# Two-layer decode attention and gated feed-forward on one core: products that nobody reads between the last values and behind them, a scaling in four pieces, row means summed beside a transpose, and 2 KB more of values kept per partition

## The chip, the cores and the metric

One NeuronCore of a Trainium2 chip runs the whole program in one launch. The metric is the device time of that launch in microseconds (us), the median of several executions. TensorE (PE in the profile) multiplies, VectorE (DVE) does elementwise work and 32x32 block transposes, ScalarE (ACT) the exponential, GpSimd (POOL) a power, and SyncE (SP) issues nearly all DMA loads.

## The reference

Two layers of the same two blocks share one set of weights and one key and value cache. There are 2 batch rows of one token, 32 query heads on 8 key/value heads of width 128, and 32768 cached positions.

```python
D, Hq, Hkv, Sk, Dh, F = 512, 32, 8, 32768, 128, 1792
def _A_ref(x, k_cache, v_cache, wq, wo):
    q = (x @ wq).reshape(B, 1, Hq, Dh).transpose(0, 2, 1, 3)
    scores = einsum("bhqd,bhkd->bhqk", q, repeat(k_cache)) * (Dh ** -0.5)
    o = einsum("bhqk,bhkd->bhqd", softmax(scores), repeat(v_cache))
    return o.transpose(0, 2, 1, 3).reshape(B, 1, Hq * Dh) @ wo
def _B_ref(x, W_gate, W_up, W_down):
    gate, up = x @ W_gate, x @ W_up
    return (gate * (gate > 0) * up) @ W_down
for layer in range(2):
    x = x + _A_ref(_layernorm(x), k_cache, v_cache, wq, wo)
    x = x + _B_ref(_layernorm(x), W_gate, W_up, W_down)
```

All arrays are f32. Keys and values are 268 MB each and are read in both layers, so that 1.1 GB pass through the DMA queues.

## The kernel before

A "head" of the kernel is one pair of key/value head and batch row: NG = 16 of them. Layer 0 goes through them upward, layer 1 downward, so that the last head of layer 0 is the first of layer 1. For each head `keys` takes 8 pages of 128x4096 keys through `k_tile` into scores, `soft_max` and `soft_tail` make weights of them, and `values` takes 8 pages of values through `v_tile` into the PSUM tile `acc`. A page of values is 8 products of 512 columns. They are written to four strips of 32 partitions of `acc` (`32 * c`), four products at a time, one for each strip. Each f32 product stands twice in a trace, since TensorE runs it in two passes.

Behind the last value of a head `evacuate` (L316) scales `acc` by one over the sum; `head_out` (L327) turns it by four small products into the tile `po` and copies it to `oT`; `project` (L338) multiplies by `wo` into `op`. Behind the last head of a layer the chain goes on: `add` (L175) forms the residual and its row sums, `centred` (L144) subtracts the mean, transposes and squares, `factor` (L156) makes the inverse deviation, and `feed_forward` (L354) multiplies by the gate and up weights (`wgu`, eight loads of 896 KB in layer 0), then by `wd`. Layer 1 begins with `queries` (L182) and eight loads of `wq`.

All loads go into one area `arena` of 220 units of 1 KB per partition (128 KB over the 128 partitions). `take` (L62) gives a load the free units that were set free first, at multiples of 8 units for the sizes here; `done` marks units as free in program order, and the load that gets them waits on the chip for the instruction that read them last. SP issues in program order, so a load that waits holds up all loads behind it.

At the end of layer 0 the area is nearly full: the 8 key pages of the last head (128 units) and of its values the pages 4 to 6 and the last quarter of page 3 (52 units) stay for layer 1, which does not load them again. `KEPT_PART, KEPT_FROM = 3, 6` says that page 3 is loaded as blocks 0 to 5 and blocks 6 and 7, and that the second part stays. Page 7 comes in four quarters. 40 units are left for all loads up to the first keys of layer 1. By `take`'s rule these make four slots of 8 units that rotate: the first four `wgu` loads get one each, and each later `wgu`, `wd` and `wq` load waits for the products on the load four places ahead of it. The first slots are those of page 3's first part (first `wgu` load), of the third and fourth quarter of page 7 (second), of the weights `pT` and of page 7's second quarter (third), and of `wo` (fourth).

Of the kernel before, what the change touches and what calls it, by code (L numbers as in the profile page):

```python
# [8 lines left out]
F32 = mybir.dt.float32  # L9
AF = mybir.ActivationFunctionType  # L10
ALU = mybir.AluOpType
AX = mybir.AxisListType
# [23 lines left out]


KEPT_PAGES = (4, 5, 6)
KEPT_PART, KEPT_FROM = 3, 6
DOWN = (4, 4, 2, 2, 1, 1)  # L40


SIDE_HEAD, SIDE_PAGE, SIDE_AT, SIDE = 12, 5, 4, 3
SIDE_ROWS, SIDE_CHUNKS = 20, 5

C_SAME, C_MEAN, C_SELH, C_PAIR, C_COL, C_SELQ, C_SIDE, C_END = 0, 128, 256, 272, 304, 306, 338, 339


@with_exitstack
def attention_reglu_decode(ctx: ExitStack, tc: tile.TileContext, x, k, v, side, wq, wo, wgu, wd, consts, out):  # L50
# [23 lines left out]
    def load(src, top=False):  # L74
        t = take(src.shape[-1], top, False)
        nc.sync.dma_start(t[0], src)
        return t

    def done(loaded):
        clock[0] += 1  # L80
        for u in loaded[1]:
            freed[u] = clock[0]
# [27 lines left out]
    selh = cst[:, C_SELH : C_SELH + 16]  # L110
    pair = cst[:, C_PAIR : C_PAIR + 32]
    selq = cst[:, C_SELQ : C_SELQ + 32]
    mean_rows = cst[:, C_MEAN : C_MEAN + P]
    side_rows = cst[:, C_SIDE : C_SIDE + 1]
    col = cst[:, C_COL : C_COL + NB]

# [13 lines left out]
    def small(name):  # L130
        return ps.tile([P, D], F32, tag="small", bufs=2, name=name)
# [1 line left out]
    ring = sb.tile([P, 32], F32, name="stat")  # L133
    turn = [0]

    def one(n=1):
        at = turn[0]
        turn[0] = (at + 2) % 32
        return ring[:, at : at + n]

    def centred(total, name):  # L144
        mp = small(f"mean{name}")
        nc.tensor.matmul(mp[:, 0:1], mean_rows, total, start=True, stop=True)  # L146
        work, xT = take(2 * P), take(P)
        xc, sq = work[0][:, :P], work[0][:, P:]
        nc.vector.tensor_scalar(xc, xq, mp[:, 0:1], None, ALU.subtract)
        nc.vector.transpose(xT[0], xc)  # L150
        ss = one()
        nc.vector.scalar_tensor_tensor(sq, xc, 1.0, xc, ALU.mult, ALU.mult, accum_out=ss)
        done(work)
        return xT, xT[0].rearrange("p (a b) -> p a b", b=32), ss

    def factor(ss, name, by_row):  # L156
        vp = small(f"var{name}")
        n = 1 if by_row else NB
        ve, rs = one(NB), one(NB)
        if by_row:  # L160
            nc.tensor.matmul(vp[:, :n], mean_rows, ss, start=True, stop=True)
        else:
            sc = one(NB)
            nc.vector.tensor_scalar_mul(sc, col, ss[:, 0:1])
            nc.tensor.matmul(vp[:, :n], mean_cols.to_broadcast([P, P]), sc, start=True, stop=True)
        nc.vector.tensor_scalar_add(ve[:, :n], vp[:, :n], EPS)
        nc.gpsimd.tensor_tensor(rs[:, :n], ve[:, :n], mhalf[:, :n], ALU.pow)
        return rs

# [4 lines left out]

    def add(tot):  # L175
        total = one()
        nc.vector.scalar_tensor_tensor(xq, tot[:, :P], 1.0, xq, ALU.mult, ALU.add, accum_out=total)
        return total


# [1 line left out]
    def queries(L, total, first, between):  # L182
        xt, xT, ss = centred(total, f"a{L}")
        qp = ps.tile([P, 2, D], F32, tag="sc", bufs=2, name=f"qp{L}")
        rq = one(NB)
        front = first // (NG // 2)
        order = [B * KT + kt for B in (front, 1 - front) for kt in range(KT)]
        parts = blocks(wq, 4 * D, order, 1 if L else 2 * KT)
        for B in (front, 1 - front):
            for kt in range(KT):  # L190
                t = next(parts)
                for c in range(4):
                    nc.tensor.matmul(qp[32 * c : 32 * c + 32, B, :], xT[:, kt, :], t[0][:, c * D : (c + 1) * D],  # L193
                                     start=kt == 0, stop=kt == KT - 1)
                done(t)
                if B != front and kt:
                    next(between, None)
                if B == front and kt == 0:
                    nc.vector.tensor_scalar_mul(rq, factor(ss, f"a{L}", False), DH ** -0.5)
            q = take(D)  # L200
            qs = q[0].rearrange("p (a b) -> p a b", b=32)
            nc.vector.transpose(q[0], qp[:, B, :])
            for b in range(NB):
                nc.vector.tensor_scalar_mul(qT[:, 16 * B : 16 * B + 16, b], qs[:, :, b], rq[:, b : b + 1])
            done(q)
            if B == front:
                place_queries(0, first)
        done(xt)
# [21 lines left out]

    def soft_max(L, n):
        m1 = one()
        nc.vector.tensor_reduce(m1, sc_of[n], AX.XY, ALU.max)  # L233
        mp = small(f"mp{L}_{n}")
        mt = take(32)
        nc.vector.tensor_scalar_mul(mt[0], pair, m1[:, 0:1])  # L236
        nc.tensor.matmul(mp[:, :32], same, mt[0], start=True, stop=True)  # L237
        done(mt)
        nm = one()
        nc.vector.tensor_reduce(nm, mp[:, :32], AX.X, ALU.max, negate=True)  # L240
        p = take(2 * D)
        rs = one()
        nc.scalar.activation(p[0], sc_of[n].rearrange("p a b -> p (a b)"), AF.Exp, bias=nm[:, 0:1], scale=1.0, accum_out=rs)  # L243
        red_of[n] = (p, rs)

    def soft_tail(L, n, aside=False):
        p, rs = red_of.pop(n)
        pT = take(2 * D)
        for B in range(2):
            nc.vector.transpose(pT[0][:, B * D : (B + 1) * D], p[0][:, B * D : (B + 1) * D])  # L250
        if aside:
            side_of[n] = side_keys(p[0])
        done(p)
        sm = small(f"sm{L}_{n}")
        nc.tensor.matmul(sm[:, 0:1], same, rs, start=True, stop=True)  # L255
        linv = one()
        nc.vector.reciprocal(linv, sm[:, 0:1])  # L257
        pT_of[n], linv_of[n] = pT, linv


# [39 lines left out]
    def v_tile(n, j, vt, first, last, blocks):  # L300
        pT = pT_of[n][0].rearrange("p (b m r) -> p b m r", m=16, r=32)
        parts = 4 // len(blocks) if len(blocks) < 4 else 1
        for at, ch in enumerate(blocks):
            J, B, m = j // 4, j // 2 % 2, j % 2 * 8 + ch
            for e in range(parts):
# [5 lines left out]
                    start=first and ch < 4, stop=last and blocks[-1] == 7 and at >= len(blocks) - 4,  # L311
                )

    acs_of = {}

    def evacuate(L, n, split):  # L316
        done(pT_of.pop(n))
        acs_of[n] = take(D)
        acs = acs_of[n][0]
        linv = linv_of.pop(n)  # L320
        if split:
            nc.vector.tensor_scalar_mul(acs[:, : D // 2], acc[:, : D // 2], linv[:, 0:1])  # L322
            nc.scalar.activation(acs[:, D // 2 :], acc[:, D // 2 :], AF.Copy, scale=linv[:, 0:1])
        else:
            nc.vector.tensor_scalar_mul(acs, acc, linv[:, 0:1])  # L325

    def head_out(L, n):  # L327
        acs = acs_of.pop(n)
        po = small(f"po{L}_{n}")
        for t in range(4):  # L330
            nc.tensor.matmul(po[:, :REP], acs[0][:, t * P : (t + 1) * P], selh[:, 4 * t : 4 * t + 4],  # L331
                             start=t == 0, stop=t == 3)
        done(acs)
        nc.vector.tensor_copy(oT[:, :, n % NB], po[:, :REP])  # L334

# [62 lines left out]
        return add(tot)  # L398

    total = one()  # L400
    nc.vector.tensor_reduce(total, xq, AX.X, ALU.add)
    kept_k, kept_v = [], []
    for L in range(NLAYER):
        last = L == NLAYER - 1
# [29 lines left out]
        def values(i, soft):  # L434
# [18 lines left out]
            for at, (j, lo, hi, t) in enumerate(pieces):  # L453
                if i == SIDE_HEAD and j == HALF:
                    aside = take(2 * SIDE_CHUNKS * D, False, False)
                    sides = load_side(L, aside)
                next(sides, None)
                next(sides, None)
                if i == SIDE_HEAD and j == NT - 1:
                    v_side(n, aside[0])  # L460
                    done(aside)
                t = t or next(whole, None) or load(v[n, j // HALF, :, j % HALF * PAGE + lo * D : j % HALF * PAGE + hi * D])
                v_tile(n, j, t[0], at == 0, j == NT - 1, range(lo, hi))
                if not last and i == NG - 1 and (j in KEPT_PAGES or j == KEPT_PART and lo):
                    kept_v.append((j, lo, hi, t))
                else:
                    done(t)
                if soft is not None and at == 0:
                    soft_max(L, soft)
            evacuate(L, n, i == NG - 1)  # L470

        first_keys = keys(0)
# [8 lines left out]
        values(NG - 1, None)  # L481
        head_out(L, seq[NG - 1])
        project(load(wo[seq[NG - 1] // NB]), NG)
        total = feed_forward(L, add(op))
    nc.sync.dma_start(out, xq)

# [58 lines left out]
```

## Time and profile before

| | us |
|---|---|
| median of 3 runs | 2578.14 (2577.77 to 2578.51) |
| the profiled execution | 2580.14 |
| its span, first to last instruction | 2578.3 |

The profiled execution stands 2.00 us above the median of the timed runs and 1.84 us above its own span. In the profile, PE is the matmul part of TensorE and PEld its weight loads; SPq is SyncE's issue of DMAs; PEclk is the share of the full 2.4 GHz that TensorE was granted, 1.00 or 0.50 at an instant and a mean over a stretch.

### The profile page before, as it was taken

Reading aid. Unit: us, or ns where it says so; the run is one execution under the profiler, and the core shown is the slowest. Engines: PE = TensorE matmul, PEld = TensorE weight load, DVE = VectorE, ACT = ScalarE, POOL = GpSimd, SP = SyncE. Lnnn points to the kernel's source line nnn. Section 1 sums busy time; section 2 is a strip of 40 time slices with the busy share of each in tenths; the row PEclk is TensorE's granted clock in tenths of the full one; section 3 lists DMA queues with packets and bytes.
Section 4 is the critical chain, followed back from the end, with each engine's and each line's share of the span. In section 5 each row is a group of like instructions: output and inputs, shape, how many; then the busy total and the mean of one; then the engine's idle time right before and its main releaser. Section 6 shows DMA issues by size and latency. Waiting matters only on the chain.

```text
span 2578.3 us, 19563 instructions
## 1 busy us (share of the span) xinstructions
PE 1306.9 (51%) x9264; PEld 337.3 (13%) x9264; DVE 147.5 (6%) x351; ACT 42.1 (2%) x69; POOL 3.4 (0%) x13
## 2 busy tenths in 40 slices
PE   2444454455445544645575554445445544554456
PEld 0111111111111111111121111111111111111111
DVE  0000000000000000000010000000000000000000
ACT  0000000000000000000000000000000000000000
POOL 0000000000000000000000000000000000000000
PEclk9777777777776777777878777767777777777778
DMA  9999999999999999999999999999999999999999
GB/s 426 427 435 435 431 432 435 431 436 431 429 439 430 431 437 429 421 436 421 424 403 434 435 434 433 434 429 435 434 428 436 434 425 440 434 431 422 436 422 391
DMA packets 31919, 1107.34 MB, mean 429 GB/s; under 512 B 3600, under 2 KB 3984, under 8 KB 7440
## 3 DMA queue, kind: packets, MB, share of 16 engines
q1 hardware_dynamic: 31552, 1105.87, 99.7%
q8 instruction: 72, 1.18, 0.2%
q10 hardware_dynamic: 288, 0.24, 0.0%
q14 instruction: 7, 0.06, 0.0%
HBM read 1106.03 MB, written 0.07 MB: 429 GB/s over the span
## 4 chain that ended last, share of the span: by engine, by line
DMA 69%; PE 22%; another core or an unknown queue 9%; issue 0%; DVE 0%; SPq 0%; ACTq 0%; DVEq 0%
DMA arena<-k 54%; PE sc L223 15%; DMA arena<-v 11%; PE acc L307 4%; DMA cst<-consts 2%; DMA arena<-wd 1%; DMA arena<-wq 1%; PE po L331 1%; PE qp L193 1%; PE op L344 0%; DMA arena<-wgu 0%; PE mp L237 0%; PE gu L362 0%; PE sm L255 0%
## 5 line engine op out<-in xcount | busy, mean ns | idle before, releaser
L223 PE MATMUL sc<-arena,qz 128*32 128x512 f32 x4096 | 592.5, 731 | 597.8 <-DMA arena<-k 597.8
L307 PE MATMUL acc<-arena 128*16 128x512 f32 (+1 forms) x4136 | 584.6, 717 | 591.8 <-DMA arena<-v 591.8
L223 PEld LDWEIGHTS sc<-arena,qz 128*32 128x32 f32 x4096 | 144.5, 131 | 1000.5 <-issue 690.5
L307 PEld LDWEIGHTS acc<-arena 128*16 128x16 f32 x4136 | 118.3, 108 | 1007.9 <-issue 506.2
L233 DVE TENSOR_REDUCE stat<-sc 128x1 f32<-128x1024 f32 x32 | 39.2, 1225 | 646.0 <-PE sc L223 646.0
L243 ACT ACTIVATE arena<-sc,stat 128x1024 f32<-128x1024 f32 x32 | 35.7, 1115 | 2372.5 <-DVE stat L240 2319.6
L325 DVE TENSOR_SCALAR arena<-acc,stat 128x512 f32<-128x512 f32 x30 | 22.5, 751 | 719.9 <-PE acc L307 719.9
L250 DVE STREAM_TRANSPOSE arena<-arena 128x512 f32<-128x512 f32 x64 | 41.5, 687 | 2.5 <-ACT arena L243 2.5
L331 PE MATMUL po<-cst,arena 128*128 128x4 f32 x256 | 34.7, 258 | 2.4 <-DVE arena L322 1.2
L331 PEld LDWEIGHTS po<-cst,arena 128*128 128x128 f32 x256 | 31.9, 195 | 27.1 <-issue 23.5
L257 DVE RECIPROCAL stat<-sm 128x1 f32<-128x1 f32 x32 | 5.3, 166 | 436.2 <-PE sm L255 436.2
L240 DVE TENSOR_REDUCE stat<-mp 128x1 f32<-128x32 f32 x32 | 6.1, 192 | 360.6 <-PE mp L237 360.6
L362 PE MATMUL gu<-arena 128*32 128x448 f32 x128 | 20.5, 751 | 12.2 <-DMA arena<-wgu 11.4
L193 PE MATMUL qp<-arena 128*32 128x512 f32 x128 | 22.1, 801 | 5.9 <-DMA arena<-wq 3.5
L146 PE MATMUL meana<-stat,cst 128*128 128x1 f32 x4 | 0.9, 304 | 43.4 <-DMA cst<-consts 43.0
L237 PEld LDWEIGHTS mp<-arena,cst 128*128 128x128 f32 x64 | 13.3, 260 | 52.5 <-issue 45.8
L237 PE MATMUL mp<-arena,cst 128*128 128x32 f32 x64 | 17.3, 358 | 3.3 <-DVE arena L236 3.3
L344 PE MATMUL op<-arena,oT 128*2 128x512 f32 x112 | 14.6, 592 | 3.6 <-DVE oT L334 3.6
L255 PEld LDWEIGHTS sm<-stat,cst 128*128 128x128 f32 x64 | 9.5, 188 | 28.8 <-issue 28.8
L255 PE MATMUL sm<-stat,cst 128*128 128x1 f32 x64 | 12.2, 260 | 0.0
L334 DVE COPY oT<-po 128x4 f32<-128x4 f32 x32 | 5.2, 161 | 78.0 <-PE po L331 78.0
L384 PE MATMUL dn<-arena 128*32 128x512 f32 x32 | 6.4, 894 | 4.3 <-DVE arena L373 3.2
(62 smaller groups left out, 85.7 us busy)
## 6 DMA issues: line engine op xcount, KB each, us to landing
arena<-v SPq DMA_DIRECT2D x31, 2048.0 KB
arena<-wo SPq DMA_DIRECT2D x16, 1024.0 KB
arena<-k SPq DMA_DIRECT2D x8, 2048.0 KB
arena<-wq SPq DMA_DIRECT2D x8, 1024.0 KB
arena<-wgu SPq DMA_DIRECT2D x8, 896.0 KB
arena<-wgu SPq DMA_DIRECT2D x4, 1792.0 KB
arena<-v SPq DMA_DIRECT2D x9, 512.0 KB
arena<-wd SPq DMA_DIRECT2D x4, 1024.0 KB
```

Source lines behind the costliest of these rows:

```text
L193: nc.tensor.matmul(qp[32 * c : 32 * c + 32, B, :], xT[:, kt, :], t[0][:, c * D : (c + 1) * D], start=kt == 0, stop=kt == KT - 1)
L223: nc.tensor.matmul(sc_of[n][32 * c : 32 * c + 32, B, :], qz[:, i % 2, 28 - 4 * j : 60 - 4 * j], kt[:, ch * D : (ch + 1) * D], start=j == 0 ...
L233: nc.vector.tensor_reduce(m1, sc_of[n], AX.XY, ALU.max)
L237: nc.tensor.matmul(mp[:, :32], same, mt[0], start=True, stop=True)
L243: nc.scalar.activation(p[0], sc_of[n].rearrange("p a b -> p (a b)"), AF.Exp, bias=nm[:, 0:1], scale=1.0, accum_out=rs)
L250: nc.vector.transpose(pT[0][:, B * D : (B + 1) * D], p[0][:, B * D : (B + 1) * D])
L255: nc.tensor.matmul(sm[:, 0:1], same, rs, start=True, stop=True)
L307: nc.tensor.matmul(acc[32 * c : 32 * c + 16, e * w : (e + 1) * w], pT[:, B, m, 16 * J : 16 * J + 16], vt[:, at * D + e * w : at * D + (e + ...
L325: nc.vector.tensor_scalar_mul(acs, acc, linv[:, 0:1])
L331: nc.tensor.matmul(po[:, :REP], acs[0][:, t * P : (t + 1) * P], selh[:, 4 * t : 4 * t + 4], start=t == 0, stop=t == 3)
L344: nc.tensor.matmul(op[32 * u : 32 * u + NB, :], oT[:, u, :], w, start=i == 3, stop=i == NG - 1)
L362: nc.tensor.matmul(gu[32 * j : 32 * j + 32, s, :FS], xT[:, kt, :], t[0][:, j * FS : (j + 1) * FS], start=kt == 0, stop=kt == KT - 1)
```

## The change

Six edits stand in it. `KEPT_FROM` goes from 6 to 5: page 3 is split after block 4, its second part (6 units instead of 4) is kept, and layer 1 loads 2 units less. `keep_busy(n, w)` is new: it issues n products of `same[:, :32]` with w columns of the first kept key page into a PSUM tile `hot` that nothing reads, always on partitions 0 to 31. It works only in layer 0, from page 4 of the last head's values on: four products of 512 columns behind each of the pages 4, 5 and 6, two of 256 behind each of the first three quarters of page 7, and one or two of 256 at four places from the last quarter on up to `centred`, which ends it. `evacuate` scales the last head's values in four pieces of 128 columns on DVE instead of two halves on DVE and ACT. `centred` and `factor` sum by column: the mean comes as a 128x2 product while DVE transposes x, and subtraction and squares work on 128x8 elements. The constants lose the 128 columns of `mean_rows`. The temporaries of `one` are all two columns wide.

```diff
-KEPT_PART, KEPT_FROM = 3, 6
+KEPT_PART, KEPT_FROM = 3, 5
...
     def centred(total, name):
         mp = small(f"mean{name}")
-        nc.tensor.matmul(mp[:, 0:1], mean_rows, total, start=True, stop=True)
-        work, xT = take(2 * P), take(P)
-        xc, sq = work[0][:, :P], work[0][:, P:]
-        nc.vector.tensor_scalar(xc, xq, mp[:, 0:1], None, ALU.subtract)
-        nc.vector.transpose(xT[0], xc)
-        ss = one()
-        nc.vector.scalar_tensor_tensor(sq, xc, 1.0, xc, ALU.mult, ALU.mult, accum_out=ss)
-        done(work)
-        return xT, xT[0].rearrange("p (a b) -> p a b", b=32), ss
+        tm, xT, sq, ss = one(), take(P), take(KT * NB), one()
+        xv = xT[0].rearrange("p (a b) -> p a b", b=32)
+        nc.vector.tensor_scalar_mul(tm, col, total[:, 0:1])
+        nc.tensor.matmul(mp[:, :NB], mean_cols.to_broadcast([P, P]), tm, start=True, stop=True)
+        keep_busy(1)
+        hot.clear()
+        nc.vector.transpose(xT[0], xq)
+        mean = bass.AP(mp.tensor, mp.offset, [mp.ap[0], [0, KT], [1, NB]])
+        nc.vector.tensor_tensor(xv[:, :, :NB], xv[:, :, :NB], mean, ALU.subtract)
+        nc.vector.tensor_tensor(sq[0].rearrange("p (a b) -> p a b", b=NB), xv[:, :, :NB], xv[:, :, :NB], ALU.mult)
+        nc.vector.tensor_reduce(ss, sq[0].rearrange("p (a b) -> p b a", b=NB), AX.X, ALU.add)
+        done(sq)
+        return xT, xv, ss
...
+    hot = []
+
+    def keep_busy(n, w=D // 2):
+        for _ in range(n if hot else 0):
+            nc.tensor.matmul(hot[0][:32, 0, :w], same[:, :32], kept_k[0][0][:, :w], start=True, stop=True)
+
...
-        if split:
-            nc.vector.tensor_scalar_mul(acs[:, : D // 2], acc[:, : D // 2], linv[:, 0:1])
-            nc.scalar.activation(acs[:, D // 2 :], acc[:, D // 2 :], AF.Copy, scale=linv[:, 0:1])
-        else:
-            nc.vector.tensor_scalar_mul(acs, acc, linv[:, 0:1])
+        for t in range(0, D, P if split else D):
+            e = t + (P if split else D)
+            nc.vector.tensor_scalar_mul(acs[:, t:e], acc[:, t:e], linv[:, 0:1])
...
         nc.vector.tensor_copy(oT[:, :, n % NB], po[:, :REP])
+        keep_busy(1)
...
+                if i == NG - 1 and not last and j >= 4:
+                    if j == 4:
+                        hot.append(ps.tile([P, 2, D], F32, tag="sc", bufs=2, name="hot"))
+                    keep_busy(*((4, D) if hi - lo == 8 else (2,) if hi < 8 else (1,)))
...
         project(load(wo[seq[NG - 1] // NB]), NG)
+        keep_busy(2)
```

On TensorE this is the end of layer 0 before: the last head's values from page 0 on (`acc`), then the chain behind them (`po`, `op`, the mean, the first gate products `gu`, the variance).

```order
L307 MATMUL acc<-arena 16x512 x30
L307 MATMUL acc<-arena 16x256 x4
L307 MATMUL acc<-arena 16x512 x24
L307 MATMUL acc<-arena 16x256 x16
L331 MATMUL po_15_2653<-cst,arena 128x4 x4
L173 MATMUL op<-arena,oT 2x128 x16
L146 MATMUL meanf_2677<-stat,cst 128x1
L362 MATMUL gu_2682<-arena 32x448 x4
L161 MATMUL varf_2688<-stat,cst 128x1
```

In this stretch of the changed kernel the pages 4, 5 and 6 and the first quarter of page 7 stand as follows (the 40 products ahead are pages 0 to 4).

```order
L311 MATMUL acc<-arena 16x512 x40
L324 MATMUL hot<-arena,cst 32x512 x4
L311 MATMUL acc<-arena 16x512 x8
L324 MATMUL hot<-arena,cst 32x512 x4
L311 MATMUL acc<-arena 16x512 x8
L324 MATMUL hot<-arena,cst 32x512 x4
L311 MATMUL acc<-arena 16x256 x4
L324 MATMUL hot<-arena,cst 32x256 x2
```

Each group of unread products (`hot`) stands ahead of the next page's values on the same engine. The second and third quarters of page 7 follow in the same form; this is TensorE's order in the changed kernel from the last quarter on.

```order
L311 MATMUL acc<-arena 16x256 x4
L324 MATMUL hot<-arena,cst 32x256
L341 MATMUL po_15_2674<-cst,arena 128x4 x4
L324 MATMUL hot<-arena,cst 32x256
L177 MATMUL op<-arena,oT 2x128 x16
L324 MATMUL hot<-arena,cst 32x256 x2
L149 MATMUL meanf_2701<-stat,ones 128x2
L324 MATMUL hot<-arena,cst 32x256
L373 MATMUL gu_2709<-arena 32x448 x4
```

The chain's own products keep their order, with one or two unread products between them. On DVE the same chain of the changed kernel reads, from the scaling on:

```order
L335 TENSOR_SCALAR arena<-acc,stat 128x128 x4
L344 COPY oT<-po_15_2674 128x4
L181 SCALAR_TENSOR_TENSOR x,stat<-op,x 128x128
L148 TENSOR_SCALAR stat<-cst,stat 128x2
L152 STREAM_TRANSPOSE arena<-x 128x128
L154 TENSOR_TENSOR arena<-arena,meanf_2701 128x4x2
```

Four pieces stand where one half stood, and the transpose now comes ahead of the subtraction. With two units more kept, `take` gives other slots at this place: the first `wgu` load gets units of page 3's first part and of the first quarter of page 7, the second those of page 7's second and third quarters, the third those of `pT`, the fourth those of `wo`. SP's order of loads stays as it was.

## Rows read from the trace of the kernel before

**Rows 1.** The page: span, bytes from memory, chain that ended last by engine.

```profile
span 2578.3 us, 19563 instructions
...
HBM read 1106.03 MB, written 0.07 MB: 429 GB/s over the span
...
DMA 69%; PE 22%; another core or an unknown queue 9%; issue 0%; DVE 0%; SPq 0%; ACTq 0%; DVEq 0%
```

**Rows 2.** The chain of waits, the program's end: start us, us, what.

```profile
2545.11 25.84 DMA arena<-wd
...
2575.39 0.29 DVE x L177
```

**Rows 3.** Busy time by stretch at the boundary; last: PEclk, DMA share, GB/s.

```profile
1284.00:1294.00 10.00, 6.50 (x70) 3.87 (x74) 1.74 (x8) 0.48 (x1) 0.00 (x0) 0.68 1.02 409
1294.00:1302.00 8.00, 5.33 (x34) 1.25 (x26) 0.16 (x1) 0.63 (x1) 0.56 (x1) 0.76 0.90 302
1302.00:1312.00 10.00, 5.76 (x36) 0.98 (x40) 1.33 (x2) 0.00 (x0) 0.00 (x0) 0.80 1.01 423
```

**Rows 4.** Timeline of PE at the end of layer 0.

```profile
1271.62 3.62 PE L307 MATMUL acc<-arena 128*16 128x512 f32 x16 [3.83 <-DMA arena<-v]
1276.51 3.61 PE L307 MATMUL acc<-arena 128*16 128x512 f32 x16 [1.28 <-DMA arena<-v]
1281.41 2.34 PE L307 MATMUL acc<-arena 128*16 128x512 f32 x24 [1.29 <-DMA arena<-v]
...
1286.57 0.62 PE L307 MATMUL acc<-arena 128*16 128x256 f32 x8 [0.70 <-DMA arena<-v]
1287.80 1.87 PE L331 MATMUL po<-cst,arena 128*128 128x4 f32 x8 [0.61 <-DVE arena L322]
1289.93 1.89 PE L173 MATMUL op<-arena,oT 128*2 128x128 f32 x32 [0.26 <-DVE oT L334]
...
1293.70 1.72 PE L362 MATMUL gu<-arena 128*32 128x448 f32 x8 [0.85 <-PE meanf L146]
...
1302.50 0.96 PE L362 MATMUL gu<-arena 128*32 128x448 f32 x8 [3.16 <-DMA arena<-wgu]
...
1308.88 0.96 PE L362 MATMUL gu<-arena 128*32 128x448 f32 x8 [0.60 <-DMA arena<-wgu]
```

**Rows 5.** Timeline of SP's load issues: all `wgu` loads, the fourth and fifth, the fifth.

```profile
1271.64 28.09 SPq L76 DMA_DIRECT2D arena<-wgu  x8
...
1291.84 3.96 SPq L76 DMA_DIRECT2D arena<-wgu  x2
...
1295.47 0.33 SPq L76 DMA_DIRECT2D arena<-wgu  x1
```

**Rows 6.** Busy time by stretch, columns as in rows 3.

```profile
1085.00:1088.00 3.00, 3.00 (x32) 0.74 (x24) 0.00 (x0) 0.00 (x0) 0.00 (x0) 1.00 1.44 617
...
1270.60:1280.60 10.00, 7.23 (x32) 0.97 (x32) 0.00 (x0) 0.00 (x0) 0.00 (x0) 0.50 0.98 417
1280.80:1287.40 6.60, 4.22 (x48) 0.99 (x48) 0.14 (x1) 0.00 (x0) 0.00 (x0) 1.00 1.04 417
1287.60:1297.60 10.00, 8.24 (x64) 4.60 (x68) 1.56 (x9) 0.48 (x1) 0.56 (x1) 0.50 0.97 374
```

**Rows 7.** Timeline of PE: the same chain at the end of layer 1.

```profile
2547.60 1.17 PE L331 MATMUL po<-cst,arena 128*128 128x4 f32 x8 [0.61 <-DVE arena L322]
2549.03 1.05 PE L173 MATMUL op<-arena,oT 128*2 128x128 f32 x32 [0.26 <-DVE oT L334]
```

**Rows 8.** Timeline of DVE: the first half's scaling, and an operation on 128x128.

```profile
1287.26 0.48 DVE L322 TENSOR_SCALAR arena<-acc,stat 128x256 f32<-128x256 f32 x1 [34.70 <-PE acc L307]
...
1292.96 0.29 DVE L149 TENSOR_SCALAR arena<-x,meanf 128x128 f32<-128x128 f32 x1 [0.75 <-PE meanf L146]
```

**Rows 9.** Timeline of PE: ten products of 512 columns on four strips (4, 4 and 2).

```profile
1085.80 2.75 PE L285 MATMUL acc<-arena 128*16 128x512 f32 x20
```

**Rows 10.** Timeline of PEld: weights of the fourth `wgu` block's first products.

```profile
1298.37 0.16 PEld L362 LDWEIGHTS gu<-arena 128*32 128x32 f32 x8 [0.82 <-DMA arena<-wgu]
```

More of the change, by code (lines that the diff above doesn't have):

```diff
@@ L44 @@
 SIDE_ROWS, SIDE_CHUNKS = 20, 5
-C_SAME, C_MEAN, C_SELH, C_PAIR, C_COL, C_SELQ, C_SIDE, C_END = 0, 128, 256, 272, 304, 306, 338, 339
+C_SAME, C_SELH, C_PAIR, C_COL, C_SELQ, C_SIDE, C_END = 0, 128, 144, 176, 178, 210, 211
 @with_exitstack
@@ L112, in attention_reglu_decode @@
     selq = cst[:, C_SELQ : C_SELQ + 32]
-    mean_rows = cst[:, C_MEAN : C_MEAN + P]
     side_rows = cst[:, C_SIDE : C_SIDE + 1]
@@ L134, in attention_reglu_decode, with one @@
     turn = [0]
-    def one(n=1):
+    def one():
         at = turn[0]
-        turn[0] = (at + 2) % 32
-        return ring[:, at : at + n]
+        turn[0] = (at + NB) % 32
+        return ring[:, at : at + NB]
     def centred(total, name):
         mp = small(f"mean{name}")
-        nc.tensor.matmul(mp[:, 0:1], mean_rows, total, start=True, stop=True)
-        work, xT = take(2 * P), take(P)
-        xc, sq = work[0][:, :P], work[0][:, P:]
-        nc.vector.tensor_scalar(xc, xq, mp[:, 0:1], None, ALU.subtract)
-        nc.vector.transpose(xT[0], xc)
-        ss = one()
-        nc.vector.scalar_tensor_tensor(sq, xc, 1.0, xc, ALU.mult, ALU.mult, accum_out=ss)
-        done(work)
-        return xT, xT[0].rearrange("p (a b) -> p a b", b=32), ss
+        tm, xT, sq, ss = one(), take(P), take(KT * NB), one()
[11 more added lines that the diff above has]
+        return xT, xv, ss
@@ L156, in factor @@
     def factor(ss, name, by_row):
         vp = small(f"var{name}")
+        ve, rs = one(), one()
         n = 1 if by_row else NB
-        ve, rs = one(NB), one(NB)
+        nc.tensor.matmul(vp[:, :NB], mean_cols.to_broadcast([P, P]), ss, start=True, stop=True)
         if by_row:
-            nc.tensor.matmul(vp[:, :n], mean_rows, ss, start=True, stop=True)
-        else:
-            sc = one(NB)
-            nc.vector.tensor_scalar_mul(sc, col, ss[:, 0:1])
-            nc.tensor.matmul(vp[:, :n], mean_cols.to_broadcast([P, P]), sc, start=True, stop=True)
@@ L166, in factor @@
-        nc.vector.tensor_scalar_add(ve[:, :n], vp[:, :n], EPS)
+            each, own = one(), one()
+            nc.vector.scalar_tensor_tensor(each, vp[:, :NB], 1.0, col, ALU.mult, ALU.mult, accum_out=own[:, :1])
+            nc.vector.tensor_scalar_add(ve[:, :1], own[:, :1], EPS)
+        else:
+            nc.vector.tensor_scalar_add(ve, vp[:, :NB], EPS)
         nc.gpsimd.tensor_tensor(rs[:, :n], ve[:, :n], mhalf[:, :n], ALU.pow)
@@ L176, in add @@
         total = one()
-        nc.vector.scalar_tensor_tensor(xq, tot[:, :P], 1.0, xq, ALU.mult, ALU.add, accum_out=total)
+        nc.vector.scalar_tensor_tensor(xq, tot[:, :P], 1.0, xq, ALU.mult, ALU.add, accum_out=total[:, :1])
         return total
@@ L184, in queries @@
         qp = ps.tile([P, 2, D], F32, tag="sc", bufs=2, name=f"qp{L}")
-        rq = one(NB)
+        rq = one()
         front = first // (NG // 2)
@@ L232, in soft_max @@
         m1 = one()
-        nc.vector.tensor_reduce(m1, sc_of[n], AX.XY, ALU.max)
+        nc.vector.tensor_reduce(m1[:, :1], sc_of[n], AX.XY, ALU.max)
         mp = small(f"mp{L}_{n}")
@@ L239, in soft_max @@
         nm = one()
-        nc.vector.tensor_reduce(nm, mp[:, :32], AX.X, ALU.max, negate=True)
+        nc.vector.tensor_reduce(nm[:, :1], mp[:, :32], AX.X, ALU.max, negate=True)
         p = take(2 * D)
         rs = one()
-        nc.scalar.activation(p[0], sc_of[n].rearrange("p a b -> p (a b)"), AF.Exp, bias=nm[:, 0:1], scale=1.0, accum_out=rs)
+        nc.scalar.activation(p[0], sc_of[n].rearrange("p a b -> p (a b)"), AF.Exp, bias=nm[:, 0:1], scale=1.0, accum_out=rs[:, :1])
         red_of[n] = (p, rs)
@@ L254, in soft_tail @@
         sm = small(f"sm{L}_{n}")
-        nc.tensor.matmul(sm[:, 0:1], same, rs, start=True, stop=True)
+        nc.tensor.matmul(sm[:, 0:1], same, rs[:, :1], start=True, stop=True)
         linv = one()
-        nc.vector.reciprocal(linv, sm[:, 0:1])
+        nc.vector.reciprocal(linv[:, :1], sm[:, 0:1])
         pT_of[n], linv_of[n] = pT, linv
@@ L400, in attention_reglu_decode @@
     total = one()
-    nc.vector.tensor_reduce(total, xq, AX.X, ALU.add)
+    nc.vector.tensor_reduce(total[:, :1], xq, AX.X, ALU.add)
     kept_k, kept_v = [], []
@@ L499 @@
     cst[:, C_SELQ : C_SELQ + NB] = np.equal.outer(rows % 32, np.arange(NB))
-    cst[:, C_MEAN : C_MEAN + P] = np.equal.outer(rows % 32, rows % 32) / D
     cst[:, C_PAIR : C_PAIR + 32] = np.equal.outer(rows // 4, np.arange(32))
```

## The prediction

> **What bounds the kernel now.** I read the page first. 1106 MB in a span of 2578.3 us are 429 GB/s, and the chain that ended last is DMA for 69% [rows 1]: the loads set the time, and a change counts only as far as it alters their bytes or lets the queue run dry. The chain of waits at the program's end confirms it: the last 25.84 us before the final products are one DMA wait, for `wd` [rows 2]. So everything in layer 1's last chain up to there, its shorter scaling and the new means, has slack and is worth nothing.
>
> Next I looked for places where the queue runs dry. Around the end of layer 0 it moves 409 GB/s until 1294, then 302 for 8 us, then 423 [rows 3]. Against 429 the 8 us lose 8 x (1 - 302/429) = 2.4 us. The timelines tell why. The last value product begins at 1286.57 and takes 0.62, so the values end at 1287.19; the first gate products begin only at 1293.70, and the fifth gate/up load, which needs the slot that these free, is issued at 1295.47 and used at 1302.50 [rows 4, 5]. In this chain TensorE's granted clock was 0.50; it had been 0.50 through pages 4 and 5 as well, 1.00 through page 6 and 7, and fell as the chain began [rows 6]. So 2.4 us is about all that a faster chain can give back.
>
> **What the change costs, part by part.**
>
> *Bytes.* Two units less in layer 1 are 0.26 MB, at 429 GB/s 0.61 us less. This is a sure gain as long as the queue is the limit. Its price is 2 units less of free area at the boundary; I count it below, through the slots.
>
> *The chain's own work.* At the higher clock the four small products take 1.17 instead of 1.87 us and the 16 of `project` 1.05 instead of 1.89 [rows 4, 7]. From the end of the values to the first gate product the chain takes 1293.70 - 1287.19 = 6.5 us; at full clock 1.5 less, 5.0. Four pieces of some 0.29 us (an operation on 128x128 [rows 8]) let the small products start after the first piece rather than after 0.48, and the last piece is ready after 1.2: about 0.1 us saved. The new mean replaces a subtraction of 0.29 by one on 128x8, with a tiny product ahead of it: nothing within 0.2 us. An unread product of 256 columns behind `po`, two behind `op`, give back some 0.2. I take 5.0, bounds 4.7 and 5.5. DVE's extra operations in `factor` lie beside three more blocks of gate products and cost nothing there; at the program's start the same operations stand ahead of the first queries, while 25.2 MB of queries' weights and keys (three loads of 64 KB per partition) are already queued, 58.7 us at 429 GB/s. They cost nothing either; without that cover it would be the same 0.2 us.
>
> *The unread products.* This is the term that decides. What does one cost? The trace has no unread product, but it has ten value products of 512 columns in sets of 4, 4 and 2 on different strips, at clock 1.00: 20 records in 2.75 us [rows 6, 9]. That is six passes of 0.43 and a drain of 0.17, and the set of two took its two passes like the sets of four. So a set's time is that of one strip, and one product alone costs 2 x 0.43 = 0.86 us. All unread products go to partitions 0 to 31, one strip: four of them cost 3.44 us, two of 256 columns 0.86. Half the clock doubles this. Bounds: 3.44 if they run one behind the other, 0.86 for all four if they could share passes as the value products do; I take the first, since nothing else in their instructions differs.
>
> [...]
>
> Pages land every 4.9 us (1271.62, 1276.51, 1281.41 [rows 4]). A page at full clock takes 4 passes x 0.43 = 1.72, with its unread products 5.16. That is more than 4.9, so TensorE falls behind, and the next values are queued behind products that nobody needs. From 1271.62 three pages end at 1271.62 + 15.48 = 1287.10; the four quarters (two passes of half width, 0.43 each) and three times 0.86 end at 1291.4. On top comes the time at half clock: page 4 begins at 0.50 [rows 6], and each us there is half lost. How long? In this trace page 4 and 5 kept TensorE 7.2 us of 10 busy and the clock stayed low until about 1280.7, whereas the gate products, which follow each other from 1293.70 nearly without a gap, ran at 0.50 until 1297.6 and a block of them at 1302.50 in 0.96 instead of 1.72 [rows 4, 6]: 4 us of work at half clock. With the unread products there is no gap either, so I take 4 us, a loss of 2.0, and as bounds 0 and the 9 us of the pages. The values then end at 1293.4 (1291.4 to 1295.9) instead of 1287.2: **6.2 us later**. The chain at full clock saves 1.5 of it.
>
> *What this does to the loads.* An issue reaches its use late: 1291.84 to 1298.37 for the fourth gate/up load and 1295.47 to 1302.50 for the fifth [rows 5, 10], 6.5 and 7.0 us. A load by itself takes 2.13 (the last four blocks are used 1302.50 to 1308.88, 3 x 2.13 [rows 4]). So 4.4 to 4.9 pass outside the queue's throughput; I take 4.5. The loads up to `wo` are issued early enough in both kernels and end near 1286.57 + 2.44 (1 MB at 429 GB/s) = 1289.0. Behind them, a load ends at the later of the previous end and issue + 4.5, plus 2.13. In the changed kernel:
> - first, after page 7's first quarter, 3 x 1.29 before the values' end: issue 1289.6, end 1296.2. Before it was issued at 1271.64 [rows 5], in time;
> - second, after the third quarter: issue 1292.2, end 1298.8; third, behind `pT`: issue 1293.5, end 1301.0;
> - fourth, behind `project`, 3.1 us after the values: issue 1296.5, end 1303.1;
> - fifth, after the first gate block (1293.4 + 5.0 + 1.0): issue 1299.4, end 1306.0. From here the queue stays full: 1308.2, 1310.3, eighth 1312.4.
>
> Before, the eighth was used at 1308.88 [rows 4]: 3.5 us later. Less the 0.61: **+2.9 us**. With the values' end at 1291.4 everything is 2.0 earlier (+0.9), at 1295.9 2.5 later (+5.4). The profiled execution of 2580.14 would become 2583.0, the median 2578.14 then **2581.0**. Layer 1's later stages move with it unchanged.
>
>
> **The rivals.**
> - *The unread products fit into the gaps.* If they cost half or less, TensorE waits for each page as before, the clock stays up, the values end by 1287.9, and the fifth load is issued near 1294, early enough for a full queue: the 2.4 us come back, with 0.61 for the bytes -3.0, 2575.1 (2575 to 2576). For it: the gap between pages, 4.9 - 1.72 = 3.2 us, is near the products' 3.44, so little is needed; it decides at a cost below 0.8 us each with the clock up at page 4. Against it: the six passes of [rows 9].
> - *A load's fixed part is short.* The 4.4 and 4.9 us may hold some waiting behind other loads. The program's last store, alone in its queue, ends 2.6 us after its data (2575.68 to 2578.3 [rows 1, 2]). With 2.4 in place of 4.5 the list above ends at 1310.3, +1.4, with the bytes +0.8: 2578.9. For it: that store. Against it: two loads of this very chain. [...]
> - *The clock stays low under the unread products.* Behind value pages it rose near 1280.7, behind gate products after 1297.6 [rows 6]; both fill four strips, an unread product one. If it stays at 0.50, a page takes 3.44 + 6.88, three pages end at 1302.6, the quarters at 1311.2, 24 us late, and the chain runs slow too; +23, 2601. If the values' own passes bring the clock back now and then, half of that, 2590. For it: no row has a stretch of products on one strip. Against it: the clock rose behind two quite different kinds of product, and in both cases after TensorE had hardly paused. It decides if PEclk reads 0.50 while the `hot` products run without a gap.
>
> **Chances.** The forecast (+0.9 to +5.4) 0.60, products in the gaps 0.17, short fixed part 0.08, slow clock 0.12, anything else 0.03. 0.2% of 2578 is 5.2 us, about what a measurement of this kernel can tell from no change. The forecast lies inside that but for its upper edge (0.04 of its 0.60), and so do the first two rivals: no change 0.81, slower 0.17 (0.04, the slow clock and 0.01 of the rest), faster 0.02, since only 2.4 + 0.6 us are there to be won. For 8 in 10 the range takes in the first rival and the forecast nearly to its upper end, 2574.8 to 2584.0, and leaves out the slow clock. The forecast's own range is 2579.0 to 2583.6.
>
> **What the profile of the changed kernel would show.** Right: the `hot` products of a page last 3.4 us at PEclk 1.00 and twice that at 0.50; page 5 and 6 begin not on a DMA but behind `hot`; the last values end near 1293; the first `wgu` load is issued behind page 7's first quarter, the DMA rate dips from about 1289 to 1297 rather than from 1294 to 1302; the chain from the values' end to the first gate product takes 5 us. Wrong: pages that still wait for their loads, or PEclk 0.50 through `hot`. The prediction fails upward if the clock stays low, and downward if the first `wgu` load is issued before 1285.

## The result, and the profile of the changed kernel

The changed kernel takes 2584.19 us (median of 15 runs, 2582.70 to 2585.99), the kernel before, on the same chip, 2578.50 us (median of 15, 2577.65 to 2581.16). The ratio is 1.002, interval 1.0013 to 1.0027, which is 3.4 to 7.0 us more: a real loss, at the edge of the 0.2% that the prediction took as its bound. Forecast were +2.9 us and 2581.0, with a range up to 2584.0; the median lies 0.2 us above that range. Measured from its own before (2578.50) the loss is 5.7 us, inside the 5.9 from 2578.14 to 2584.0 but above the +5.4 at which the forecast itself ended. The execution shown here took 2583.93 us.

The page of the changed kernel still shows a kernel that loads bound:

```profile
span 2582.2 us, 19657 instructions
HBM read 1105.70 MB, written 0.07 MB: 428 GB/s over the span
DMA 66%; PE 24%; another core or an unknown queue 9%; DVE 0%; issue 0%; SPq 0%; ACTq 0%; DVEq 0%
```

It reads a little less than before [rows 1] in a span 3.9 us longer. The place is found in the windows, in stretches around the end of layer 0 (busy us of PE, PEld, DVE, ACT and POOL with the number of instructions, then TensorE's granted clock, DMA share, GB/s):

```profile
1284.00:1294.00 10.00, 9.95 (x66) 3.58 (x58) 0.54 (x3) 0.00 (x0) 0.00 (x0) 1.00 0.72 254
1294.00:1302.00 8.00, 6.83 (x76) 3.58 (x76) 2.30 (x14) 0.00 (x0) 0.56 (x1) 1.00 0.92 335
...
1271.80:1272.80 1.00, 1.00 (x12) 0.31 (x16) 0.00 (x0) 0.00 (x0) 0.00 (x0) 1.00 0.96 410
1273.20:1276.20 3.00, 3.00 (x11) 0.59 (x4) 0.00 (x0) 0.00 (x0) 0.00 (x0) 0.50 0.98 415
1276.60:1300.00 23.40, 23.35 (x168) 8.88 (x165) 2.84 (x15) 0.00 (x0) 0.22 (x1) 1.00 0.85 317
...
1288.50:1290.50 2.00, 2.00 (x19) 0.90 (x15) 0.00 (x0) 0.00 (x0) 0.00 (x0) 1.00 0.00 0
...
1290.50:1302.00 11.50, 10.28 (x104) 5.15 (x102) 2.84 (x15) 0.00 (x0) 0.56 (x1) 1.00 0.95 326
```

Before, the first stretch moved 409 and the second 302 GB/s [rows 3]; now the first moves 254 and the second 335. From 1288.50 to 1290.50 the queue moves nothing at all, and from there to 1302.00 it moves 326. TensorE is busy for 9.95 of the 10 us in which the loads run dry, and at the full granted clock. The timeline of TensorE says with what (start and length in us, engine, line, operation; a group counts from its first record's start to its last one's end, so one row can reach into the next; each f32 product is two records, called passes here):

```profile
1271.75 2.43 PE L311 MATMUL acc<-arena 128*16 128x512 f32 x16 [3.86 <-DMA arena<-v]
1273.94 4.40 PE L324 MATMUL hot<-arena,cst 128*32 128x512 f32 x7
...
1278.18 0.59 PE L324 MATMUL hot<-arena,cst 128*32 128x512 f32 x1
1278.19 2.29 PE L311 MATMUL acc<-arena 128*16 128x512 f32 x13
1280.33 3.17 PE L324 MATMUL hot<-arena,cst 128*32 128x512 f32 x7
1282.91 0.61 PE L311 MATMUL acc<-arena 128*16 128x512 f32 x3
1283.33 0.59 PE L324 MATMUL hot<-arena,cst 128*32 128x512 f32 x1
1283.35 2.29 PE L311 MATMUL acc<-arena 128*16 128x512 f32 x13
1285.47 3.17 PE L324 MATMUL hot<-arena,cst 128*32 128x512 f32 x7
...
1292.59 0.79 PE L311 MATMUL acc<-arena 128*16 128x256 f32 x4
1293.87 1.16 PE L341 MATMUL po<-cst,arena 128*128 128x4 f32 x8
...
1297.89 1.04 PE L373 MATMUL gu<-arena 128*32 128x448 f32 x8
...
1301.30 0.96 PE L373 MATMUL gu<-arena 128*32 128x448 f32 x8 [1.17 <-DMA arena<-wgu]
1303.48 1.54 PE L373 MATMUL gu<-arena 128*32 128x448 f32 x8 [1.22 <-DMA arena<-wgu]
...
1312.23 1.72 PE L373 MATMUL gu<-arena 128*32 128x448 f32 x8 [0.45 <-DMA arena<-wgu]
```

Only page 4 waits for its load (`[3.86 <-DMA arena<-v]`); pages 5 and 6 stand behind `hot` without a wait, 5.16 us apart (1278.19, 1283.35), where pages land every 4.9. The values end at 1292.59 + 0.79 = 1293.38 instead of 1287.19, and the eighth gate/up block is used at 1312.23 instead of 1308.88 [rows 4]. SP's issues of the first five gate/up loads follow TensorE, one after the other:

```profile
1289.57 0.33 SPq L76 DMA_DIRECT2D arena<-wgu  x1
1292.17 0.33 SPq L76 DMA_DIRECT2D arena<-wgu  x1
1293.49 0.33 SPq L76 DMA_DIRECT2D arena<-wgu  x1
1296.49 0.33 SPq L76 DMA_DIRECT2D arena<-wgu  x1
1299.01 0.33 SPq L76 DMA_DIRECT2D arena<-wgu  x1
```

Before, the first of them was issued at 1271.64 [rows 5], ahead of everything that is late now. The chain of waits through the same stretch has the unread products on it, and then a load:

```profile
1283.92 1.72 PE acc L311 x13
1285.64 2.81 PE hot L324 x7
...
1296.49 6.94 DMA arena<-wgu
```

A chain that holds `hot`, whose result nobody reads, is the finding in one line: passes of unread products are steps of their own in the chain that ends in the late load.

### The profile page after: what moved, and what is told of

The parts are those of the page before. It is cut to its first block, busy times and chain, and to the rows that moved or that the text cites. A ratio compares the mean times of both kernels' runs of the same rounds, so it can differ in the third digit from the quotient of the medians.

```text
span 2582.2 us, 19657 instructions
## 1 busy us (share of the span) xinstructions
PE 1317.8 (51%) x9302; PEld 342.5 (13%) x9302; DVE 149.2 (6%) x363; ACT 41.1 (2%) x67; POOL 3.4 (0%) x13
## 4 chain that ended last, share of the span: by engine, by line
DMA 66%; PE 24%; another core or an unknown queue 9%; DVE 0%; issue 0%; SPq 0%; ACTq 0%; DVEq 0%
DMA arena<-k 50%; PE sc L227 16%; DMA arena<-v 12%; PE acc L311 5%; DMA cst<-consts 2%; DMA arena<-wgu 1%; PE po L341 1%; PE qp L197 1%; DMA arena<-wq 1%; PE hot L324 1%; PE op L355 0%; PE gu L373 0%; PE sm L259 0%; PE mp L241 0%
## 5 line engine op out<-in xcount | busy, mean ns | idle before, releaser
L335 DVE TENSOR_SCALAR arena<-acc,stat 128x512 f32<-128x512 f32 (+1 forms) x38 | 24.8, 665 | 785.3 <-PE acc L311 785.3
L324 PE MATMUL hot<-arena,cst 128*32 128x512 f32 (+1 forms) x46 | 18.0, 520 | 0.0
```

Source lines behind the costliest of these rows:

```text
L324: nc.tensor.matmul(hot[0][:32, 0, :w], same[:, :32], kept_k[0][0][:, :w], start=True, stop=True)
L335: nc.vector.tensor_scalar_mul(acs[:, t:e], acc[:, t:e], linv[:, 0:1])
```

## The experiments

The theory was that of the prediction: unread products on one strip run one behind the other, delay the last values, and with them the issues of the gate/up loads. Rivals were that another part of the change (the means, the scaling, the bytes) costs the time, that any unread product costs it, and, since the loss was larger than the sum, that the sum's price of the delay was too low. The means, scaling and kept values are in all kernels made from the changed one, and no run leaves out a part of the computation that is read. Ratios are to the kernel before on the same chip.

**Each half alone.** `e1_no_products` is the changed kernel without the block that starts the unread products, so that none is ever made; `e2_products_only` is the kernel before with all of the unread products and nothing else of the change.

```diff
 # e1: left out; e2: added to the kernel before, with keep_busy and its calls in the chain
-                if i == NG - 1 and not last and j >= 4:
-                    if j == 4:
-                        hot.append(ps.tile([P, 2, D], F32, tag="sc", bufs=2, name="hot"))
-                    keep_busy(*((4, D) if hi - lo == 8 else (2,) if hi < 8 else (1,)))
```

> The changed kernel without any unread product; the other edits stay (2 KB more kept and so the other slots, four pieces, means by column). Theory of the delay (the products hold up the last values): those are done near 1287 us again, and the time is that of the kernel before less the 0.6 us of bytes, ratio 0.9995 to 1.0000. Rival of the slots (the first gate/up load comes later because its slot now covers a quarter of page 7): still slower than before by 2 us or more, ratio over 1.0008. Rival of the new chain (four pieces and column means cost more than they save): also over 1.0008, with the chain from the last value to the first gate product longer than 6.5 us.

> The kernel before with the unread products alone; old slots, old means, two halves. Theory of the delay: the last values end near 1293 to 1294, the ratio is that of the whole change or 0.0002 more, 1.0018 to 1.0028. Rival of the slots: the first gate/up load is issued near 1271 as before, the queue is fed, and the ratio is 1.0008 or less. Rival of the new chain: 1.0008 or less.

Without the products: 2577.09 us, 0.9996 (0.9988 to 1.0005). With the products alone: 2585.08 us, 1.0026 (1.0016 to 1.0036). The loss is whole in the second and gone in the first. In the windows 1284 to 1302 the first moves 403 GB/s:

```profile
1284.00:1302.00 18.00, 14.11 (x120) 5.06 (x112) 2.85 (x15) 0.63 (x1) 0.56 (x1) 0.68 1.01 403
```

The second moves 288, and its SP timeline shows that the free area of 2 units does not matter beside the products. The first gate/up load is issued at 1271.70, as in the kernel before, and the next one still waits for the values:

```profile
1271.70 0.33 SPq L76 DMA_DIRECT2D arena<-wgu  x1
1293.38 0.33 SPq L76 DMA_DIRECT2D arena<-wgu  x1
```

So the means, the scaling and the bytes together are worth nothing that 11 runs can tell (-3.1 to +1.3 us), and the unread products cost about 7 us: 2584.19 - 2577.09 = 7.1, 6.7 if each is first taken against its own before, and 6.9 by the second run (2585.08 - 2578.14).

**The same products on four strips.** `e4_four_strips` makes as many unread products in each place, the products of a group on partitions 0, 32, 64 and 96 in turn.

```diff
-        for _ in range(n if hot else 0):
-            nc.tensor.matmul(hot[0][:32, 0, :w], ...
+        for c in range(n if hot else 0):
+            nc.tensor.matmul(hot[0][32 * c : 32 * c + 32, 0, :w], ...
```

> The changed kernel with the same number of unread products, but each group spread over the four strips of 32 partitions instead of all on the first. Theory that one strip makes them run in a row: a group of four takes 0.86 us instead of 3.44, pages no longer wait behind products, the last values end near 1287 to 1288, ratio 0.9985 to 1.0000. Rival that a product costs its time wherever it is written: the group still takes 3.4 us and the ratio is 1.0015 or more.

2578.03 us, 1.000 (0.9991 to 1.0009). TensorE's timeline shows a group of four at half clock, 1.79 us, and at full clock, 1.03 us with its drain (the 0.17 us or so by which a row outlasts its passes of 0.43), and page 6 that waits for its load again:

```profile
1274.88 1.79 PE L324 MATMUL hot<-arena,cst 128*32 128x512 f32 x8
...
1278.22 1.03 PE L324 MATMUL hot<-arena,cst 128*32 128x512 f32 x8
1281.29 1.91 PE L311 MATMUL acc<-arena 128*16 128x512 f32 x16 [2.04 <-DMA arena<-v]
```

The number of products is the same, only the strip differs, and the loss is gone. This is the direct test of the step on which the sum stood: four products on one strip take 3.44 us, on four strips a quarter. The Trainium skill, page "TensorE: Matmul & The Clock Gate", section "What picks the tile position", says that the output's start partition is the column tile; the two runs agree: products with one start partition ran one behind the other, and products with four start partitions ran together.

**Products where nothing is delayed.** `e3_chain_only` starts the products behind the last quarter of page 7, so only the chain has them. `e12_late_only` has one of 256 columns behind each quarter of page 7 and those of the chain, none behind the pages.

```diff
 # e3
-                if i == NG - 1 and not last and j >= 4:
-                    if j == 4:
-                        hot.append(...)
-                    keep_busy(*((4, D) if hi - lo == 8 else (2,) if hi < 8 else (1,)))
+                if i == NG - 1 and not last and hi == 8 and j == NT - 1:
+                    hot.append(...)
+                    keep_busy(1)
 # e12
+                if i == NG - 1 and not last and j >= 7:
+                    if lo == 0:
+                        hot.append(...)
+                    keep_busy(1)
```

> The changed kernel with unread products only behind the last quarter of page 7 and in the chain, none between the values. Theory of the delay: the last values end near 1287 as before; the ratio is 0.9985 to 1.0000 according to whether the clock is up in the chain. If the products in the chain alone cost the time (they stand ahead of the chain's own small products), it is over 1.0008.

> The changed kernel with one unread product of 256 columns behind each quarter of page 7 and those of the chain, none behind whole pages. Theory of the delay: a quarter with its product takes 0.86 us, less than the 1.27 between quarters, so nothing is late; the clock is up in the chain, the queue stays full, ratio 0.9988 to 0.9998. Rival that any product ahead of the last values costs: 1.0004 or more.

2577.26 us, 0.9996 (0.9987 to 1.0005), and 2577.62 us, 0.9995 (0.9986 to 1.0004). Both chains run at the higher clock (first gate products at 1291.42 and 1291.35), and both move 420 GB/s in the 18 us, here `e12_late_only`:

```profile
1284.00:1302.00 18.00, 12.94 (x126) 5.17 (x122) 2.84 (x15) 0.63 (x1) 0.56 (x1) 0.94 1.02 420
```

The queue stays nearly full, and the medians stand only 0.4 and 0.5 per mille, about 1.2 us, below the kernel before. The intervals reach 1.4 per mille, 3.6 us, so that the prediction's first limit, 2.4 us for the whole dip, is not contradicted.

**The kept values alone.** `e8_kept_only` is the kernel before with

```diff
-KEPT_PART, KEPT_FROM = 3, 6
+KEPT_PART, KEPT_FROM = 3, 5
```

> The kernel before with the 2 KB more of values kept and nothing else. By the prediction the bytes give 0.6 us, the slots cost nothing while TensorE is on time: ratio 0.9995 to 1.0000, the gate/up loads issued near 1285, 1286, 1287. Rival of the slots: 1.0005 or more.

2577.33 us, 0.9995 (0.9986 to 1.0004). The bytes' 0.61 us cannot be told from nothing here, and neither can any harm that the 2 units less of free area do by themselves.

**Three products, and eight.** `e5_three_and_one` puts three behind a page and one of 256 columns behind each quarter; `e7_eight` puts eight behind a page.

```diff
-                    keep_busy(*((4, D) if hi - lo == 8 else (2,) if hi < 8 else (1,)))
+                    keep_busy(*((3, D) if hi - lo == 8 else (1,)))                         # e5
+                    keep_busy(*((8, D) if hi - lo == 8 else (2,) if hi < 8 else (1,)))     # e7
```

> The changed kernel with three unread products of 512 columns behind a page instead of four, and one of 256 behind a quarter of page 7 instead of two, all on one strip. Theory of the delay with 0.86 us a product: a page with its products takes 1.72 + 2.58 = 4.3 us, less than the 4.9 between pages, so what the slow start costs is caught up; the last values end near 1287 to 1288, the ratio is 0.9990 to 1.0003, 5 us or more below the whole change. Rival that any products between the values cost the same (by the slots or by contention): 1.0015 or more.

> The changed kernel with eight unread products of 512 columns behind each of the pages 4, 5 and 6 instead of four. Theory of the delay: twelve products more at 0.86 us, 10.3 us more before the last values end (near 1304), and as the queue is dry by then, 9 to 11 us more in the end, ratio 1.0055 to 1.007. Rival that the loads still hide part of it: under 1.0045.

Eight: 2593.90 us, 1.0058 (1.0045 to 1.0072). Its TensorE timeline has pages with 6.6 us of `hot` each, and the values' last sums (`po`) at 1303.62, 9.75 us later than in the changed kernel:

```profile
1291.79 6.60 PE L324 MATMUL hot<-arena,cst 128*32 128x512 f32 x15
...
1303.62 1.16 PE L341 MATMUL po<-cst,arena 128*128 128x4 f32 x8
...
1322.64 1.72 PE L373 MATMUL gu<-arena 128*32 128x448 f32 x8 [0.44 <-DMA arena<-wgu]
```

The eighth gate/up block is 10.4 us later (1322.64 - 1312.23). In time the 9.75 us cost 9.71 (2593.90 - 2584.19), or 9.1 with each kernel taken against its own before; the two intervals leave some 4 us either way. With the queue dry, a us of delay costs about a us.

Three: 2581.22 us, 1.0010 (1.0001 to 1.0019). This expectation failed. With three products a page needs 1.72 + 2.58 = 4.30 us, less than the 4.9 between pages, and I expected the values to end in time and the loss to be gone. The timeline of TensorE shows where that was wrong:

```profile
1276.98 2.29 PE L311 MATMUL acc<-arena 128*16 128x512 f32 x13
...
1281.19 0.61 PE L311 MATMUL acc<-arena 128*16 128x512 f32 x3
1281.26 0.59 PE L324 MATMUL hot<-arena,cst 128*32 128x512 f32 x1
1281.62 1.94 PE L311 MATMUL acc<-arena 128*16 128x512 f32 x13
1283.40 2.31 PE L324 MATMUL hot<-arena,cst 128*32 128x512 f32 x5
...
1285.55 0.59 PE L324 MATMUL hot<-arena,cst 128*32 128x512 f32 x1
...
1288.37 0.79 PE L311 MATMUL acc<-arena 128*16 128x256 f32 x4
...
1289.64 1.16 PE L341 MATMUL po<-cst,arena 128*128 128x4 f32 x8
```

Page 6 begins at 1281.19, not later than before, where it began at 1281.41 with a wait for its load [rows 4]. But these are three passes, as many as there are free strips; the last `hot` pass of page 5 begins at 1281.26, so that the strip of the unread products is free only at about 1281.69. Up to there three products nearly fit: half a us of the slow start is left. And behind page 6 no page lands; the next loads are the quarters of page 7, and the same timeline of `e12_late_only` shows when they are there:

```profile
1283.68 0.62 PE L311 MATMUL acc<-arena 128*16 128x256 f32 x8
1284.96 0.62 PE L311 MATMUL acc<-arena 128*16 128x256 f32 x8 [0.23 <-DMA arena<-v]
1286.23 0.63 PE L311 MATMUL acc<-arena 128*16 128x256 f32 x8 [0.24 <-DMA arena<-v]
```

The second quarter is used at 1283.68 there; in `e5_three_and_one` page 6 and its products hold that strip for 4.30 us, to 1285.98 (the last `hot` pass begins at 1285.55). Four quarters of 0.43 with three products of 0.43 between them then end at 1289.0, with the drain at 1289.16, where they did end (1288.37 + 0.79), 2 us late. Half a us of this is the slow start; with page 6 punctual the same count gives 1288.7, still 1.5 late. So even at full clock and with every page in time, products behind page 6 delay the end of the values. The eighth block is used at 1308.14; until the first scores of layer 1 have their maximum 2 us more are lost, which I cannot assign.

**How much the boundary itself varies.** One trace of before was the base of the sum. Three more, `e6_before_again`, `e10_before_third` and `e11_before_fourth`, and a second of the changed kernel, `e9_after_again`, are the same kernels profiled again, without an edit.

> The kernel before once more, for a second trace. The measured difference of 5.7 us is 2.8 more than predicted. Theory that the profiled execution was an unlucky one (the clock half through the whole chain): here the eighth gate/up block is used at 1306 to 1307.5 instead of 1308.9 and the span is 2576 to 2577. Rival that the surplus is elsewhere in the changed kernel: 1308.5 or later again, span near 2578.

> The changed kernel once more, for a second trace. Theory that the forecast of its boundary is right and the misfit lies in the kernel before: the last values end within 1 us of 1293.4 and the first scores' maximum of layer 1 is taken within 1.5 us of 1353.9. Rival that the first trace of the changed kernel was a lucky one: 2 us or more later.

> The kernel before, third trace. In the first the first scores' maximum of layer 1 is taken at 1350.8, in the second at 1349.2. Theory that the first was unlucky at the boundary: 1348.0 to 1349.7. Rival that it is typical: 1350.3 or later.

> The kernel before, fourth trace, with the same two numbers: 1348.0 to 1349.7 if the first was unlucky, 1350.3 or later if it is typical.

TensorE's timeline has the eighth gate/up block of the three executions of before at

```profile
1307.27 1.72 PE L362 MATMUL gu<-arena 128*32 128x448 f32 x8 [0.45 <-DMA arena<-wgu]
```

```profile
1306.39 1.67 PE L362 MATMUL gu<-arena 128*32 128x448 f32 x8 [0.66 <-DMA arena<-wgu]
```

```profile
1307.71 1.70 PE L362 MATMUL gu<-arena 128*32 128x448 f32 x8 [0.46 <-DMA arena<-wgu]
```

and of the second of the changed kernel at

```profile
1311.72 1.72 PE L373 MATMUL gu<-arena 128*32 128x448 f32 x8 [0.46 <-DMA arena<-wgu]
```

In the first trace of before it was 1308.88 [rows 4], the latest of four. Between 1284 and 1302 that trace moved 361 GB/s, the others 389, 411 and 394; by 18 x (1 - x/429) they lost 2.9, 1.7, 0.8 and 1.5 us. The two traces of the changed kernel moved 290 and 293, a loss of 5.8 and 5.7. So the base of the sum was an execution with the largest loss seen. The three later expectations came true: the values of `e9_after_again` end at 1293.13, and layer 1's first maximum is taken at 1353.69 there, at 1348.07 in `e10_before_third` and at 1349.04 in `e11_before_fourth`. `e6_before_again` fell short of its expectation at the end: its boundary was 1.6 us better than the first, and its span, 2579.7, still 1.4 longer, lost in later stages. The part of the span behind layer 1's first maximum differs between executions of before by 3.0 us (1227.5 to 1230.5), about as much as was sought.

## Why the prediction was right in its mechanism and short in its size

- **An unread product costs 0.86 us on one strip; a page with four 5.16.** Right to the hundredth: 1278.19 to 1283.35. `e4_four_strips` shows the cause.
- **The clock.** Predicted were 4 us at half clock from page 4 on, a loss of 2.0, and then full clock. Measured: 1.00 from 1271.8 to 1272.8, 0.50 from 1273.2 to 1276.2, 1.00 from 1276.6 through the products and the chain. That is 3.0 to 3.8 us at half clock, a loss of 1.5 to 1.9, though it fell only after page 4 had begun. The prediction's remark that the clock had risen in both rows after TensorE had hardly paused does not fit its first row: up to 1280.6 TensorE was busy for 7.23 of 10 us [rows 6]. The rival in which products on one strip leave the clock low falls with the row 1276.60:1300.00.
- **The values end at 1293.4.** They ended at 1293.38, in the second trace at 1293.13. That it fits to the hundredth is luck: the loss at half clock was somewhat smaller than taken, and the drain of the last pass and a start 0.13 us later (1271.75 against 1271.62) made up for it.
- **The issues at 1289.6, 1292.2, 1293.5, 1296.5 and 1299.4.** Measured 1289.57, 1292.17, 1293.49, 1296.49, 1299.01.
- **The chain takes 5.0 us from the values' end to the first gate product.** 1297.89 - 1293.38 = 4.5: 0.5 better than taken, below the bound of 4.7. It saves 2.0, not 1.5, of the delay.
- **A load's fixed part of 4.5 us.** The list of ends held: the fourth load has 1303.1 in it and lasts from 1296.49 to 1303.43 in the chain of waits. The rival with 2.4 gives 1301.0 for it and 1310.3 for the eighth, and its time falls with them. That 4.5 us are a fixed part is not shown. The 6.94 us of the fourth load less 2.13 are 4.8, but the third load was still ahead of it: its products begin at 1301.30, and those of the fourth 2.18 later, one load's share. The first load, into an empty queue, was issued at 1289.57, and bytes moved from about 1290.5, a us later. From there to 1302.00 the queue moved 326 GB/s, not 429, so 3.75 MB; four loads are 3.67 MB, and the fourth was used at 1303.48, some 1.7 us after its last bytes if the loads move in order (an estimate from these rows). So the 4.5 stands for a start, an end and a slower queue together, and that the list came out as it did is in part luck.
- **The eighth block at 1312.4.** 1312.23 and 1311.72, as listed.
- **"Before, the eighth was used at 1308.88: 3.5 us later."** This is the term that was mis-sized. Its first number is one execution's; the mean of the other three is 1307.12, and with that the term is 1312.4 - 1307.1 = 5.3, with the bytes +4.7, inside the measured +3.4 to +7.0. By the traces alone the eighth block is 4.4 us later (means 1311.98 and 1307.56), and the executions profiled took 3.9 us longer (means 2583.86 and 2579.94). The rest up to the medians' 5.7 lies within the interval. It is not settled whether part of this rest is a loss in later stages; the scatter there, 3.0 us, hides it. There was a warning ahead of the prediction: this execution stood 2.00 us above the median. That alone does not tell a bad boundary, since `e6_before_again` took 1.3 us more (2581.46) with a better one.
- **Products that fit into the gaps** (the rival that gains): false for one strip. On four strips it comes true, with values that end at 1287.07, and yet the ratio is 1.000, not the 3 us gained that this rival named. Its 2.4 us were those of the first trace of before; in the other three the 18 us lost 1.3 on the mean.

None of the variants beats the kernel before clearly: the best, `e8_kept_only` and `e12_late_only`, stand at 0.9995 with intervals that reach from 0.9986 to 1.0004.

## What to carry to other kernels

Work that nobody reads is not free where needed work stands behind it on the same engine: price it by the strip it uses and compare the sum with the interval at which the next real operands land, load by load, since here it shrinks from 4.9 to 1.3 us at the very end. If such products are wanted, spread them over four strips or put them behind the last real product, and look first at what a faster chain can give at most, here under 3 us of 2578. When a sum of a few us replaces a stretch of one profiled execution, take that stretch from several executions, because the same stretch of the same program lost 0.8 to 2.9 us here.

## What the runs showed of the hardware

- The granted clock stayed at 1.00 while TensorE ran products on a single strip of 32 columns and nothing else, in `e7_eight` for 5.8 us in one piece (the row below). In the changed kernel it was 1.00 from 1276.6 to 1300, where the four traces of before stand at 0.67 to 0.81 on the mean of 1284 to 1302.
- Passes on other strips can start before a row of unread ones has ended: three of the next page's begin at 1282.91, 0.42 us before the last `hot` pass at 1283.33. That is one pass; it does not shorten the row of four.
- Behind a queue that had run empty, bytes moved again about 1 us after the issue (1289.57, 1290.5), and for the next 11.5 us at 326 GB/s instead of 429. Why it was slower with few loads queued is not shown.

The window of `e7_eight` in which only `hot` products run:

```profile
1292.00:1297.80 5.80, 5.80 (x14) 1.43 (x13) 0.00 (x0) 0.00 (x0) 0.00 (x0) 1.00 0.00 0
```
